# A forward scan moved ahead of the key product in a blocked linear attention, and weight splits and a sort moved ahead of the second expand group

## The chip, the cores and the metric

The kernel runs on one core of one Trainium2 chip. The metric is the device time of one execution in microseconds (us). A core has five engines with their own instruction streams: TensorE (PE, matrix products; PEld are its weight loads), VectorE (DVE), ScalarE (ACT), GpSimd (POOL) and SyncE (SP, which issues DMAs here). They wait for each other by semaphores.

## The reference, cut to what matters

Two stages in sequence. The first is a linear attention with a decaying state, for 4 batches, 8 heads, 768 steps and a head size of 48; the second a mixture of 8 experts in which each of the 3072 tokens goes to one.

```python
state = 0
for t in range(768):
    cur = einsum('bhd,bhe->bhde', u * k[t], v[t])
    y[t] = einsum('bhd,bhde->bhe', r[t], state + cur)
    state = w[t][..., None] * state + einsum('bhd,bhe->bhde', k[t], v[t])
x = y as [3072 tokens, 384]
logits = x @ w_gate
e = argmax(logits); g = softmax(logits)[e]
out = g * (relu(x @ w1[e]) @ w2[e])      # w1 384x1024, w2 1024x384
```

## The kernel before, in words

**Stage one, 24 blocks.** Time is cut into 12 chunks of 64 steps, and each chunk into two blocks (two batches each). A block holds 8 segments of 64 steps, so its tiles are 112 partitions by 512 columns. For block n VectorE makes two running products of the decay: a forward scan `pre` (`dve_pre`, L346, the scan at L351), whose segment ends are inverted by a small reciprocal (L354), and a backward scan `suf` (`dve_suf`, L356, the scan at L360), which reads those ends. Then `kh` = k times `suf` (`dve_kh`, L364, product at L368, VectorE) and `rh` = r times `pre` (`pool_rh`, L389, product at L393, GpSimd) feed TensorE: `pe_a` (L457) multiplies kh and rh into `ap`, and VectorE copies the part below the diagonal into `at` under a mask (`dve_at`, L370, L373). `at` times v is added to rh times the carried state (`pe_inter`, `pe_av`), and the state takes kh transposed times v (`pe_kt`, `act_kt`, `pe_dp`). GpSimd also makes `rk` = r times k (L387) and, from ScalarE's column `ct`, half of the diagonal of `at` (`pool_diag`, L421; ScalarE makes the other half, L430).

**The order.** The order of each engine is written out by hand: `iteration(n)` (L707) emits block n's products and the parts of blocks n+1 and n+2 that are made ahead, and each engine runs what it is given in that order. For VectorE one iteration is: `suf` of n+1; in every fourth iteration the gate or the place of a group of four blocks; `at` of n; `kh` of n+1; `pre` and its reciprocal for n+2. For GpSimd: `rh` of n+1, `rk` of n+2, from iteration 6 on the scatter of 128 finished tokens by an indirect DMA (L603), the diagonal of n+1, and once in four the copy of token numbers (L598). In iteration 3 GpSimd also builds a list of small constants (`late_constants`, L192).

**Routing.** As groups of four blocks are done, the gate's logits are taken (`logit_mm`, `logit_tr`, `gate`), each token's row among its expert's is counted on TensorE (`rank`, L568, its running base copied by ScalarE at L580) and turned into a row number (`place`, L582, VectorE), and the token is scattered to that row of `xs` in HBM. The expert with the most tokens is chosen early (`choose`) and is computed first; its first 256 rows (`ua`) come from groups that were counted by then, the other 208 (`ub_`) are loaded later. The order of the rest follows from a sort of the counts (`sort_experts`, L630: five small VectorE operations), and SP reads the second expert's number from its result (`expert_of`, L691) before it issues that expert's loads.

**The tail of stage one.** After the loop (from L854) the last block's products, the row transposes of `ua`, the last ranks and scatters and the first expert's expand groups are interleaved by hand. An expand group `mm1(ua, f)` (`expand`, L304) is nine products into one bank, a ScalarE relu `hh` (L313) and a VectorE residual `hl` (L314). Weights are split into a high and a low part before use: `side(0)` (L806) takes the next piece in a list and calls `split_part` (L230), a ScalarE copy (L237) and a VectorE subtraction (L239) on 128 x 512. For one expert the list has six pieces of w1, of which the first three serve f = 0 to 3 and the other three f = 4 to 7, then six of w2. When all pieces of a load are split, `feed` (L790) issues the next load. Then `contract` (L317) multiplies the eight `hh`, `hl` pairs with w2, 24 products to an output slice, and VectorE scales the slice (L330). After that comes the second part of the first expert, and then seven experts in the same way.

Of the kernel before, what the change touches and what calls it, by code (L numbers as in the profile page):

```python
# [22 lines left out]
NB = NS * 2  # L23
# [32 lines left out]
def rwkv_moe_kernel(ctx, tc, rkw, vv, ub, wg, wr, w1, w2, out):  # L56
# [18 lines left out]
    def work(shape, dtype, tag, name=None):  # L75
        return wk.tile(shape, dtype, name=name or tag, tag=tag, bufs=WKB[tag])
# [14 lines left out]
    def misc(name):  # L91
        return psM.tile([P, BANK], F32, name=name, tag="m")
# [241 lines left out]
    def prefill(e):  # L334
        nc.sync.dma_start(xs[e, LEAST:CMAX, :].rearrange("(p j) c -> p (j c)", j=ZJ), zrow[:(CMAX - LEAST) // ZJ])
# [4 lines left out]
    def real(n):  # L340
        return 0 <= n < NB
# [1 line left out]
    def part(j):  # L343
        return slice(64 * j, 64 * j + (64 if j == 0 else D))

    def dve_pre(n):  # L346
        if real(n):
            d = blk[n]
            d["pt"] = pre_[n % 2]
            d["pre"] = d["pt"][:, 0, 0:NW].rearrange("p (m c) -> p m c", c=SEG)  # L350
            nc.vector.tensor_tensor_scan(out=d["pt"][:, 0, 0:NW], data0=d["w"], data1=cell[:RP, 0:1].broadcast_to([RP, NW]),  # L351
                                         initial=1.0, op0=ALU.mult, op1=ALU.min)
            src = d["pt"][:, :, C + 1:C + 1 + NW].rearrange("p o (m c) -> p o m c", c=SEG)[:, :, :, 0]
            nc.vector.reciprocal(d["ends"], src.rearrange("p o m -> p m o"))  # L354

# [8 lines left out]
    def dve_kh(n):  # L364
        if real(n):
            d = blk[n]
            d["kh"] = work([RP, NSEG, C], F32, "kh")
            nc.vector.tensor_tensor(out=d["kh"], in0=d["k"], in1=d["suf"][:, :, 3:SEG], op=ALU.mult)  # L368
# [34 lines left out]
    def act_g(n):  # L403
        if real(n) and n >= 2:
            p = n % 2
            nc.scalar.activation(gst[p], U[:RP, p, 0:NSEG * D], AF.Copy)
# [115 lines left out]
    def pe_xT(n, t):  # L522
        if real(n):
            G, i = divmod(n, GRP)
            blk[n]["xp"] = xp = t[:, 0:DM]
            for j in range(3):
                nc.tensor.transpose(xp[:, j * P:(j + 1) * P], ch["xr", G][:, i, j * P:(j + 1) * P], ident)  # L527
# [12 lines left out]
    def logit_tr(k):  # L540
        lt = misc("lt")[:, 0:32 * k[2]]
        nc.tensor.transpose(lt, ch["ls"], ident[0:32 * k[2], 0:32 * k[2]])
        ch["lp", k] = lt.rearrange("p (b e) -> p b e", e=32)[:, :, 0:E]
# [24 lines left out]
    def rank(k):  # L568
        G, i, m = k
        oh = ch["r", k][0]  # L570
        t = misc("rank")
        rk = t[:, 0:(m + 1) * E].rearrange("p (b e) -> p b e", e=E)
        ch["rank", k] = rk
        nc.tensor.matmul(rk, one32, ch["base"].unsqueeze(1).broadcast_to([1, m + 1, E]), start=True, stop=False, skip_group_check=True)
        nc.tensor.matmul(rk[:, 0:m], tri, oh, start=False, stop=False, skip_group_check=True)
        for b in range(m):
            nc.tensor.matmul(rk[:, b + 1:], ones, oh[:, b:b + 1, :].broadcast_to([P, m - b, E]),
                             start=False, stop=(b == m - 1), skip_group_check=True)
        ch["base"] = nb = sm.tile([1, E], F32, name="base", tag="base", bufs=3)
        nc.scalar.activation(nb, rk[0:1, m, :], AF.Copy)  # L580
# [126 lines left out]
    def iteration(n):  # L707
        G, i = divmod(n, GRP)
        g = G - 1 if n >= 0 else -1
        whole = (g, 0, GRP)  # L710
        if 0 <= n < E // 2:
            prefill(2 * n)
            prefill(2 * n + 1)
        if n >= 0:
            load(n + 6)
        full = 0 <= g < NG - 1
        if real(n):
            blk[n]["ap"] = psA.tile([P, 4, 256], F32, name="ap", tag="ap")
            pe_xT(n - 1, blk[n]["ap"][:, 1:3, :].rearrange("p a c -> p (a c)"))
            pe_inter(n)  # L720
            if full and i == 1:
                logit_tr(whole)
            pe_a(n)
            if n == 0:
                zeros(blk[n]["yp"][:, 1, NQ * D:], 3)
        dve_scale(n + 1)
        act_pend(n + 1)
        act_g(n + 1)
        pool_rh(n + 1)
        dve_suf(n + 1)  # L730
        if full and i == 1:
            gate(whole)
        if full and i == 2:
            place(whole)
        if n == -2:
            pool_rk(0)
        pe_kt(n)
        act_pad(n + 2)
        if n == NB - 2:
            dve_kh(n + 1)  # L740
            dve_at(n)
            side()
        else:
            dve_at(n)
            dve_kh(n + 1)
        act_kt(n)
        act_ct(n + 1)
        if n > -2:
            pool_rk(n + 2)
        pe_av(n)  # L750
        if full and i == 0:
            act_xT(n - 1)
            logit_mm(whole)
        if n < 2:
            act_diag(n + 1, range(0, H if n < 0 else NQ))
        if n == NB - 2:
            dve_diag(n + 1)
            act_xT(n - 1)
            act_xr(n)
        else:  # L760
            act_xr(n)
            if not (full and i == 0):
                act_xT(n - 1)
        if 2 <= n < NB - 2:
            act_diag(n + 1, range(0, NQ))
        if moved(n) and n < NB - 2:
            scatter(*moved(n), ch["lp"] if full and i == 0 else ch["av"])
        if n >= 0:
            pool_diag(n + 1)
        dve_pre(n + 2)  # L770
        pe_dp(n)
        if n >= 0:
            load_v(n + LV)
        if n == FIRST * GRP + 6:
            choose()
            eid[0] = expert_of(first[0:1, 0:1])
            feed()
        if full and i == 1:
            weigh(whole)
            pool_ids(g)  # L780
            rank(whole)
        if n == 3:
            late_constants()
# [22 lines left out]
    def side(limit=E):  # L806
        if sides and sides[0][1] <= limit:
            kind, e, i, t, p, done = sides.pop(0)
            if kind == "split":
                split_part(wts[e % 2], t, i, p)  # L810
            else:
                check_w(e - 1, t, p)
            if done:
                out_.remove((e, i))
                feed()
# [33 lines left out]
    with tc.manual_schedule(engines={ET.PE, ET.DVE, ET.Activation, ET.Pool}):  # L849
# [6 lines left out]
        ua, z = ch["ua"], NB - 1  # L856
# [27 lines left out]
        def mm1(u, f):  # L884
            expand(wts[u["e"] % 2], f, u["x"], u["n"], u["hs"])
# [7 lines left out]
        penalty()  # L893
        scatter(last, (0, 1, 2))
        mm1(ua, 0)
        rank(kb)
        weigh(kb)
        place(kb)
        scatter(last, (3,))
        side(0)  # L900
        mm1(ua, 1)
        side(0)
        mm1(ua, 2)
        side(0)
        sort_experts()
        eid[1] = expert_of(order[0:1, 0:1])
        ub_ = rows_of(HB, HA, 0)
        feed()
        for f in range(3, 8):
            mm1(ua, f)  # L910
            side(0)
            if f == 5:
                check_counts()
        actx.close()
# [299 lines left out]
```

## Time and profile before

| | |
|---|---|
| median of 3 runs | 391.16 us (390.44 to 392.19) |
| the profiled execution's own time | 389.0 us |
| span of the profiled execution, first to last instruction | 387.3 us |
| mean granted TensorE clock | 0.974 |
| busy: PE / PEld / DVE / ACT / POOL | 360.6 / 326.1 / 261.6 / 196.0 / 143.8 us |
| chain that ended last, share by engine | PE 80%, DVE 7%, ACT 4%, issue 3%, POOL 2% |
| DMA | 67.63 MB, mean 175 GB/s |

The profile shows one execution. The chain is followed back from the last instruction: at each step to what released it, or to the instruction before it on its engine. A row of the timeline gives start (us from the span's start), duration (us), engine, line, operation, output<-inputs, form, count, and in brackets the engine's idle time before it with what ended it. A row of windows gives the busy time of each engine in a stretch, and the granted clock (PEclk; 1.00 is 2.4 GHz, 0.50 is 1.2 GHz). A row by line gives the count, total busy time, mean ns of one, idle time before them and what ended it. Matmul ends are modelled, so a busy TensorE is not TensorE at its peak.

### The profile page before, as it was taken

The numbers are of one execution on the slowest core, as the hardware profiler recorded it, in microseconds if no ns is written. First come the engines' busy times: TensorE is split into PE (matmuls) and PEld (weight loads), VectorE is DVE, ScalarE is ACT, GpSimd is POOL, SyncE is SP. The second block draws the span as 40 slices with busy tenths as digits, with TensorE's granted clock in tenths as the row PEclk, the third lists the DMA queues.
The fourth block names the chain that finished last, engine by engine and source line by source line (L and its number), as shares of the span: only waits on it lengthen the run. The fifth ranks groups of instructions, "written<-read, shape, count | busy, mean of one in ns | idle before, by whom it ended". The sixth has DMA issues, their size and how long they took to land.

```text
span 387.3 us, 11609 instructions
## 1 busy us (share of the span) xinstructions
PE 360.6 (93%) x4644; PEld 326.1 (84%) x4645; DVE 261.6 (68%) x451; ACT 196.0 (51%) x516; POOL 143.8 (37%) x195
## 2 busy tenths in 40 slices
PE   7988999999998896999999999999999999999991
PEld 5666777777776675998998999999999999999990
DVE  8789999989998436595665376476476585782410
ACT  3665666566666234374454355465565563751200
POOL 5577688788887171111000130130130262124021
PEclk9999999999999696999999999999999999999996
DMA  7997777677768125977444554754764665811001
GB/s 205 261 276 215 225 209 225 202 218 220 221 179 278 50 111 146 284 244 239 117 164 162 151 155 149 224 161 154 226 172 146 208 164 187 248 70 40 20 19 41
DMA packets 38021, 67.63 MB, mean 175 GB/s; under 512 B 8141, under 2 KB 19714, under 8 KB 37962
## 3 DMA queue, kind: packets, MB, share of 16 engines
q1 hardware_dynamic: 31658, 57.33, 50.2%
q0 software_dynamic: 6304, 9.50, 7.7%
q8 instruction: 38, 0.62, 0.7%
q14 instruction: 21, 0.17, 0.1%
HBM read 55.34 MB, written 11.64 MB: 173 GB/s over the span
## 4 chain that ended last, share of the span: by engine, by line
PE 80%; DVE 7%; ACT 4%; issue 3%; POOL 2%; another core or an unknown queue 1%; DMA 1%; POOLq 0%; DVEq 0%; ACTq 0%
PE N L311 15%; PE N L325 14%; PE cell L311 7%; PE mM L311 6%; PE N L994 6%; PE cell L994 4%; PE mM L994 3%; PE yp L489 3%; PE yp L479 3%; PE ap L464 2%; DVE kh L368 2%; PE U L499 2%; PE N L300 2%; PE ap L527 2%; PE wrm L142 2%
## 5 line engine op out<-in xcount | busy, mean ns | idle before, releaser
L275 POOL DMA_INDIRECT out_dram<-ot,gi x16 | 22.2, 1391 | 104.0 <-issue 71.7
L275 POOL DMA_INDIRECT out_dram<-ort,gi x13 | 15.5, 1195 | 76.9 <-issue 19.3
L325 PE MATMUL N<-w2h,hh 128*128 128x384 f32 (+4 forms) x104 | 35.9, 345 | 0.0
L314 DVE SCALAR_TENSOR_TENSOR hl<-N,hh 128x256 fp32r<-128x256 f32 (+8 forms) x38 | 19.8, 522 | 23.7 <-ACT hh L313 21.9
L325 PE MATMUL N<-w2l,hh 128*128 128x384 f32 (+4 forms) x104 | 35.0, 337 | 0.0
L325 PE MATMUL N<-w2h,hl 128*128 128x384 f32 (+4 forms) x104 | 35.0, 337 | 0.0
L239 DVE TENSOR_TENSOR w2l<-wst,w2h 128x512 fp32r<-128x512 f32 x48 | 32.1, 687 | 4.1 <-ACT w2h L237 3.6
L239 DVE TENSOR_TENSOR w1l<-wst,w1h 128x512 fp32r<-128x512 f32 x48 | 33.1, 690 | 1.4 <-ACT w1h L237 1.0
L387 POOL TENSOR_TENSOR rk<-rkwt 112x512 f32<-112x512 f32 x24 | 30.6, 1275 | 7.8 <-DMA rkwt<-in_rkw_dram 7.8
L603 POOL DMA_INDIRECT xs<-xr,pi x24 | 24.7, 1028 | 23.8 <-issue 7.3
L313 ACT ACTIVATE hh<-N 128x256 fp32r<-128x256 f32 (+8 forms) x38 | 17.6, 464 | 27.0 <-PE N L311 22.4
L360 DVE TENSOR_TENSOR_SCAN suf<-rkwt,cell 112x536 f32<-112x536 f32 x24 | 30.4, 1267 | 0.5
L237 ACT ACTIVATE w2h<-wst 128x512 fp32r<-128x512 f32 x48 | 28.5, 625 | 3.5 <-DMA wst<-in_w_dram 3.5
L351 DVE TENSOR_TENSOR_SCAN pre<-rkwt,cell 112x536 f32<-112x536 f32 x24 | 30.2, 1259 | 0.2 <-DMA rkwt<-in_rkw_dram 0.2
L237 ACT ACTIVATE w1h<-wst 128x512 fp32r<-128x512 f32 x48 | 29.8, 623 | 0.2 <-ACT x L301 0.2
L393 POOL TENSOR_TENSOR rh<-rkwt,pre 112x512 f32<-112x512 f32 x24 | 28.9, 1203 | 2.3 <-DVE pre L351 2.0
L311 PE MATMUL N<-xh,w1h 128*128 128x440 f32 (+6 forms) x84 | 28.8, 343 | 0.0
L311 PE MATMUL N<-xh,w1l 128*128 128x440 f32 (+6 forms) x84 | 28.6, 341 | 0.0
L311 PE MATMUL N<-xl,w1h 128*128 128x440 f32 (+6 forms) x84 | 28.6, 340 | 0.0
L368 DVE TENSOR_TENSOR kh<-rkwt,suf 112x512 f32<-112x512 f32 x24 | 28.4, 1181 | 0.0
L430 ACT ACTIVATE at<-id,ct 128x64 f32<-128x64 f32 x96 | 25.3, 343 | 0.1
L373 DVE COPY_PREDICATED at<-cmask,ap 128x512 f32<-128x512 int32 x24 | 17.6, 735 | 10.2 <-PE ap L464 7.6
(200 smaller groups left out, 967.5 us busy)
## 6 DMA issues: line engine op xcount, KB each, us to landing
wst<-in_w_dram SPq DMA_DIRECT2D x48, 256.0 KB
wst<-in_w_dram SPq DMA_DIRECT2D x16, 768.0 KB
rkwt<-in_rkw_dram SPq DMA_DIRECT2D x72, 96.0 KB
rkwt<-in_rkw_dram SPq DMA_DIRECT2D x24, 238.0 KB
vt<-in_vv_dram SPq DMA_DIRECT2D x48, 96.0 KB
wck_t<-in_wr_dram SPq DMA_DIRECT2D x6, 768.0 KB
rkwt<-in_rkw_dram SPq DMA_DIRECT2D x12, 224.0 KB
xg<-xs SPq DMA_DIRECT2D x4, 579.0 KB
```

Source lines behind the costliest of these rows:

```text
L237: nc.scalar.activation(hi, st[:, cs], AF.Copy)
L239: nc.vector.tensor_tensor(out=lo, in0=st[:, cs], in1=hi.bitcast(F32), op=ALU.subtract)
L275: i = nc.gpsimd.indirect_dma_start(out=out[:, :], out_offset=bass.IndirectOffsetOnAxis(ap=t.bitcast(I32)[0:rows.shape[0], q, 1:2], axis=0) ...
L311: nc.tensor.matmul(hp, a, x[p][:, j, :], start=(i == 0), stop=(i == 8))
L325: nc.tensor.matmul(op, a[:, cs], w2v(wt, w, f), start=(i == 0), stop=(i == 23))
L351: nc.vector.tensor_tensor_scan(out=d["pt"][:, 0, 0:NW], data0=d["w"], data1=cell[:RP, 0:1].broadcast_to([RP, NW]), initial=1.0, op0=ALU.mu ...
L360: nc.vector.tensor_tensor_scan(out=suf[:, ::-1], data0=d["w"][:, ::-1], data1=cell[:RP, 0:1].broadcast_to([RP, NW]), initial=1.0, op0=ALU. ...
L368: nc.vector.tensor_tensor(out=d["kh"], in0=d["k"], in1=d["suf"][:, :, 3:SEG], op=ALU.mult)
L387: nc.gpsimd.tensor_tensor(out=d["rk"], in0=d["r"], in1=d["k"], op=ALU.mult)
L393: nc.gpsimd.tensor_tensor(out=d["rh"], in0=d["r"], in1=d["pre"][:, :, 1:C + 1], op=ALU.mult)
L430: nc.scalar.activation(d["at"][:, h // NQ, h % NQ, :], id2, AF.Copy, scale=d["ct"][:, h:h + 1])
L994: nc.tensor.matmul(pp, w, a, start=(i == 0), stop=(i == 23))
```

## The change

In `iteration`, for n from 2 to 21, VectorE's `kh` of block n+1 moves behind the forward scan of block n+2: `at`, scan, `kh`, reciprocal instead of `at`, `kh`, scan, reciprocal. The other engines' orders in the loop stay as they are. In the tail, three calls of `side(0)` (the three pieces of w1 that serve f = 4 to 7) move from between the expand groups 1 to 3 to behind `mm1(ua, 0)`, ahead of the last rank; and the sort, the reading of the second expert's number, the load of `ub_` and the `feed` move ahead of expand group 1. Nothing is computed otherwise than before.

```diff
--- before.py
+++ after.py
@@ -343,13 +343,16 @@
     def part(j):
         return slice(64 * j, 64 * j + (64 if j == 0 else D))
 
-    def dve_pre(n):
+    def dve_pre(n, m):
         if real(n):
             d = blk[n]
             d["pt"] = pre_[n % 2]
             d["pre"] = d["pt"][:, 0, 0:NW].rearrange("p (m c) -> p m c", c=SEG)
             nc.vector.tensor_tensor_scan(out=d["pt"][:, 0, 0:NW], data0=d["w"], data1=cell[:RP, 0:1].broadcast_to([RP, NW]),
                                          initial=1.0, op0=ALU.mult, op1=ALU.min)
+        if 2 <= m < NB - 2:
+            dve_kh(m + 1)
+        if real(n):
             src = d["pt"][:, :, C + 1:C + 1 + NW].rearrange("p o (m c) -> p o m c", c=SEG)[:, :, :, 0]
             nc.vector.reciprocal(d["ends"], src.rearrange("p o m -> p m o"))
 
@@ -742,7 +745,8 @@
             side()
         else:
             dve_at(n)
-            dve_kh(n + 1)
+            if n < 2:
+                dve_kh(n + 1)
         act_kt(n)
         act_ct(n + 1)
         if n > -2:
@@ -767,7 +771,7 @@
             scatter(*moved(n), ch["lp"] if full and i == 0 else ch["av"])
         if n >= 0:
             pool_diag(n + 1)
-        dve_pre(n + 2)
+        dve_pre(n + 2, n)
         pe_dp(n)
         if n >= 0:
             load_v(n + LV)
@@ -893,22 +897,20 @@
         penalty()
         scatter(last, (0, 1, 2))
         mm1(ua, 0)
+        for _ in range(3):
+            side(0)
         rank(kb)
         weigh(kb)
         place(kb)
         scatter(last, (3,))
-        side(0)
-        mm1(ua, 1)
-        side(0)
-        mm1(ua, 2)
-        side(0)
         sort_experts()
         eid[1] = expert_of(order[0:1, 0:1])
         ub_ = rows_of(HB, HA, 0)
         feed()
-        for f in range(3, 8):
+        for f in range(1, 8):
             mm1(ua, f)
-            side(0)
+            if f > 2:
+                side(0)
             if f == 5:
                 check_counts()
         actx.close()
```

## Rows read from the trace of the kernel before

**Rows 1.** Windows: busy us of each engine in three stretches, granted clock, DMA
```profile
core 0: us, PE busy (x) PEld busy (x) DVE busy (x) ACT busy (x) POOL busy (x), PEclk, DMA share, GB/s
47.90:120.20 72.30, 68.57 (x1935) 54.46 (x1927) 68.08 (x98) 47.01 (x165) 58.41 (x74) 1.00 0.73 212
...
149.05:155.88 6.83, 6.18 (x26) 5.74 (x27) 5.95 (x19) 4.09 (x11) 0.00 (x0) 0.50 0.54 181
156.80:182.00 25.20, 25.20 (x175) 24.74 (x174) 17.51 (x34) 13.63 (x30) 3.38 (x4) 1.00 0.84 261
```

**Rows 2.** Windows, line L368 (kh) alone: busy us and count on DVE
```profile
47.90:120.20 72.30, 17.67 (x14) 1.00 0.73 212
```

**Rows 3.** Groups by line, VectorE: forward scan and masked copy
```profile
L351 DVE TENSOR_TENSOR_SCAN pre<-rkwt,cell 112x536 f32<-112x536 f32 x24 | 30.2, 1259 | 0.2 <-DMA rkwt<-in_rkw_dram 0.2
...
L373 DVE COPY_PREDICATED at<-cmask,ap 128x512 f32<-128x512 int32 x24 | 17.6, 735 | 10.2 <-PE ap L464 7.6 <-ACT at L430 1.5 <-ACT ex L565 1.0
```

**Rows 4.** Timeline of a steady block (n = 11), VectorE and GpSimd
```profile
68.67 0.74 DVE L373 COPY_PREDICATED at<-cmask,ap 128x512 f32<-128x512 int32 x1 [0.24 <-PE ap L464]
...
69.03 1.27 POOL L387 TENSOR_TENSOR rk<-rkwt 112x512 f32<-112x512 f32 x1
...
69.31 1.54 DVE L368 TENSOR_TENSOR kh<-rkwt,suf 112x512 f32<-112x512 f32 x1
...
70.58 1.17 POOL L603 DMA_INDIRECT xs<-xr,pi  x1 [0.28 <-PE yp L489]
```

**Rows 5.** Timeline of iterations 3 and 4, VectorE and GpSimd
```profile
28.44 1.26 DVE L351 TENSOR_TENSOR_SCAN pre<-rkwt,cell 112x536 f32<-112x536 f32 x1
...
29.83 0.29 POOL L194 TENSOR_SCALAR_AFFINE_SELECT tri<-tri 128x128 bf16<-128x128 bf16 x1
...
31.99 1.17 POOL L393 TENSOR_TENSOR rh<-rkwt,pre 112x512 f32<-112x512 f32 x1
...
32.30 3.20 DVE L368 TENSOR_TENSOR kh<-rkwt,suf 112x512 f32<-112x512 f32 x1
...
33.13 1.26 POOL L387 TENSOR_TENSOR rk<-rkwt 112x512 f32<-112x512 f32 x1
...
34.35 0.60 POOL L421 TENSOR_TENSOR at<-id,ct 128x256 f32<-128x256 f32 x1
...
35.43 1.25 DVE L351 TENSOR_TENSOR_SCAN pre<-rkwt,cell 112x536 f32<-112x536 f32 x1
...
36.77 1.19 POOL L393 TENSOR_TENSOR rh<-rkwt,pre 112x512 f32<-112x512 f32 x1 [1.81 <-DVE pre L351]
```

**Rows 6.** Timeline of iteration 5, VectorE and GpSimd
```profile
38.60 0.74 DVE L373 COPY_PREDICATED at<-cmask,ap 128x512 f32<-128x512 int32 x1
...
39.23 0.69 DVE L368 TENSOR_TENSOR kh<-rkwt,suf 112x512 f32<-112x512 f32 x1
...
40.27 0.61 POOL L421 TENSOR_TENSOR at<-id,ct 128x256 f32<-128x256 f32 x1 [1.09 <-ACT ct L411]
...
40.83 0.19 POOL L598 COPY xr<-tokid 128x4 int32<-128x4 int32 x1
```

**Rows 7.** Timeline of the tail, from the last rank's base to the first scaled slice
```profile
145.05 0.17 ACT L580 ACTIVATE base<-rank 1x8 f32<-1x8 f32 x1 [3.22 <-PE N L311]
...
148.74 0.38 ACT L313 ACTIVATE hh<-N 128x256 fp32r<-128x256 f32 x1 [3.01 <-remote]
...
149.16 0.42 DVE L314 SCALAR_TENSOR_TENSOR hl<-N,hh 128x256 fp32r<-128x256 f32 x1 [2.70 <-ACT hh L313]
...
149.70 0.80 PE L311 MATMUL N<-x,w1h 128*128 128x256 f32 x2 [2.80 <-ACT w1h L237]
...
156.78 0.34 PE L325 MATMUL N<-w2h,hh 128*128 128x384 f32 x1
...
157.97 1.29 DVE L239 TENSOR_TENSOR w2l<-wst,w2h 128x512 fp32r<-128x512 f32 x2
...
161.15 0.62 DVE L330 TENSOR_SCALAR ort<-N,gi 128x384 f32<-128x384 f32 x1 [1.88 <-PE N L325]
```

**Rows 8.** Waits of SP's queue, 110 to 160 us: total, times, longest
```profile
SPq L692 <- DVE order L637: 5.3, 1, 5.3
```

## The prediction

> **What bounds the kernel now.** The chain that ended last lies mostly on TensorE, and next on VectorE (the table ahead has the shares), so time is won only where TensorE waits, or where VectorE hands it work late. Next I read busy time by stretch [rows 1]. Through blocks 8 to 21 of the loop (47.9 to 120.2 us) VectorE is busy 68.08 and TensorE 68.57 of 72.30 us: two engines in step, neither with much to give. At 149.05 to 155.88 the granted clock is 0.50, so TensorE runs at 1.2 GHz instead of 2.4. From 156.8 to 182 TensorE is busy the whole 25.20 us, so what starts that stretch earlier moves the end by as much. In the same blocks fourteen products that make the keys (kh) take 17.67 us [rows 2], 1.26 each, while a single one takes 0.69 [rows 6]; the forward scan takes 1259 ns on average [rows 3].
>
> The timeline of a steady block tells why [rows 4]. GpSimd's product rk runs 69.03 to 70.30; VectorE's kh starts at 69.31 and ends at 70.85, 0.55 after rk. kh stands still while GpSimd multiplies; scans keep their length. Where GpSimd issues products back to back, kh waits for all of them [rows 5]: started at 32.30 it sat through rh, rk and the diagonal and ended at 35.50, again 0.55 after the last (34.95).
>
> **The change, part by part.** The sum is made against the profiled execution, 389.0 us (span 387.3); the median of the runs is 391.16, so I add 2.16 at the end.
>
> Part one, steady blocks. No instruction is added or removed; kh swaps places with a scan of 1.26 us. kh would be asked for some 1.9 us after the start of the masked copy (at) instead of 0.64: in [rows 4] at 70.57, when rk is done and GpSimd is at its scatter, so it takes about 0.69 there. Over the fourteen the excess is 17.67 - 14 x 0.69 = 8.0 us [rows 2]. That is the upper end, as if VectorE alone set the pace. It does not: at already waits for the attention products in 7.6 of its 10.2 idle us [rows 3], and TensorE is idle only 72.30 - 68.57 = 3.7 us [rows 1]. The lower end is 0: TensorE keeps its pace. I take 3.0, near TensorE's idle time, because TensorE is late next. What waits behind the later kh: the reciprocal, then the backward scan, on VectorE; the attention products of the next block on TensorE, two us later in [rows 4] than kh's end, so covered. The scan asks earlier for a column that ScalarE pads; a tenth of a us a block at most, as an estimate, inside this range.
>
> Part one, first blocks. The first scatter comes in iteration 6; before it GpSimd has nothing between a diagonal and the next rh but a wait for the scan: rh at 36.77 waited 1.81 us for the scan of 35.43 [rows 5]. Moving that scan forward removes the wait, so GpSimd runs on without a gap, and kh, now behind the scan, meets the whole run. Iteration 4: the scan runs 32.30 to 33.56; kh asks while rk is running (33.13 to 34.39); the diagonal follows to 34.95, then rh (1.19) to 36.1 and the next rk (1.26) to 37.4; kh ends at 37.9. Before, kh and scan were both done at 36.68: 1.2 us lost. Iteration 5 [rows 6]: the diagonal starts 1.67 after at (38.60), held by ScalarE's ct, not by VectorE. The new kh asks 0.63 + 1.25 = 1.88 after at, 0.2 too late to be first. Diagonal, token copy, rh and rk last 0.61 + 0.19 + 1.19 + 1.26 = 3.25; kh ends 1.67 + 3.25 + 0.55 = 5.5 after at, where kh and scan now end 1.32 + 1.25 = 2.5 after it: 3.0 lost, and the next at waits for it through kh, backward scan and place. Sum: 4.2 lost. In iterations 2 and 3 I count 0: small operations there should let kh in. Bounds: a gain of 1.4 (case a) to a loss of 9.4 (case c).
>
> Here a rule weighs against the row. The Trainium skill, page "SBUF — State Buffer", section "Who interferes with whom", says a VectorE instruction with two SBUF inputs contends with a GpSimd instruction that reads SBUF, and that whoever issues first keeps the pair for the whole instruction. By it kh would lose to one instruction only; the row of 32.30 shows three, and I go by the row.
>
> Part two, the tail. Three splits (each a ScalarE copy and a VectorE subtraction, some 0.65 apiece) and the sort (small VectorE operations) move ahead of the second expand group. Now ScalarE idles 3.22 us until 145.05 and 3.01 until 148.74, the first behind TensorE; VectorE gets its next residual at 149.16, and TensorE waits 2.80 for a split of w1 until 149.70, then runs at half clock [rows 7, 1]. After: the splits lie in ScalarE's and VectorE's first idle time (142 to 145), so groups four and five follow at once and no split of w1 stands between the residuals. If the two late results stay late, VectorE has from 149.16 seven residuals (0.42) and six splits of w2 (0.645, from the pair of 1.29): 6.8 us, to 156.0. The last six of the 24 products of the first output slice come after that. A product takes (161.15 - 156.78) / 24 = 0.18, so the slice is scaled at 157.1 instead of 161.15 [rows 7]. Gain 4.0. If the late results come in time too, VectorE starts some 3 us sooner: gain up to 7. Lower end 0: the waits come back at group six, which needs a bank that the residual of group one frees. I take 4.0, nearest to the rows as they stand.
>
> Moved queues: SP waits 5.3 us for the sort's order [rows 8]; behind it stand the second row load, then the second expert's weights. They go out some 4 us earlier, which I cost at nothing, as TensorE is never short of data from 156.8 on [rows 1]. GpSimd's last scatter waits for a place that now stands behind three splits; with that result seen at 145.05 anyway it costs 0; if not, 2 us under the contraction's cover.
>
> **Sum:** -3.0 + 4.2 - 4.0 = -2.8. 389.0 - 2.8 = 386.2 profiled, 388.3 as the median.
>
> **The rivals.** (a) GpSimd's products let kh in between them: iteration 4 ends at 34.39 + 0.55 = 34.95 instead of 36.68 (1.7 gained), iteration 5 loses 0.3; the first blocks gain 1.4 instead of losing 4.2: 382.7. Against it: kh behind three [rows 5]. For it: that run was a backlog after a list of small constants. Chance 0.17. The page's rule above would give this.
>
> (b) The tail gives nothing, since the two late results only move to the next instruction that needs them: -3.0 + 4.2 = +1.2, 392.3. For it: ScalarE's 3.01 us has no releaser that the profile names [rows 7]. Against it: the splits need no result of TensorE. Chance 0.2.
>
> (c) Slower: the same blocking in iteration 3. There small constants (one of 0.29 at 29.83 that reads SBUF) follow the diagonal, then rh at 31.99 and rk to 34.39 [rows 5]. If these hold kh off as well, it ends at 34.95, where kh and scan now end at 29.70: 5.2 more, 393.5. It decides if kh, asking at about 29.2, finds no gap up to 31.99. Against it: the constants are short. Chance 0.13.
>
> (d) The swap does nothing in steady blocks because TensorE keeps its pace: 388.3 + 3.0 = 391.3. Chance 0.08.
>
> **How the numbers follow.** The forecast has 0.42. 0.5%, about what a measurement of this kernel tells from no change, is 2.0 us: faster is below 389.2, slower above 393.1. Faster: 0.36 of the forecast's 0.42 (its bounds spread it by 2 us either way), all 0.17 of (a), 0.03 of (b) and (d): 0.56. Slower: half of (c), a third of (b), 0.02 of the rest: 0.15. Same: 0.29. The range goes from (a) to just short of (c): 382.7 to 393.0.
>
> **What would show it.** Right: kh near 0.7 from iteration 7 on, beside scatters; kh of over 3 us in iterations 4 and 5; at waiting for attention products in most steady blocks; no wait of 2.80 us at the fourth group; the first output slice scaled about 4 us earlier against the end of the loop. Wrong: kh short everywhere (a), one of some 5 us in iteration 3 (c), TensorE still idle before the contraction (b).

## The result, and the profile after

The changed kernel takes 390.56 us (median of 21 runs, 383.31 to 396.55), the kernel before 391.16 in its three first runs and 391.2 over the 21 taken beside it. The ratio is 0.9896, with a 95% interval of 0.9861 to 0.9932: about 4 us faster by that ratio. The ratios here count only the runs within 1.5% of the fastest of their own kernel, here 9 of 21 after and 16 of 21 before, and so lean on how fast that fastest one happened to be: over all 21 runs the medians differ by 0.6 us only, the means by 2.0. The profiled execution went from 389.0 to 386.4 us, its span from 387.3 to 384.7.

Cut into stages, the 2.6 us of the two spans are a sum of large terms with opposite signs. "at(n)" is the start of VectorE's masked copy of block n; every boundary is read from a timeline.

| stage | before | after | difference |
|---|---|---|---|
| start to at(0) | 12.6 | 13.1 | +0.5 |
| at(0) to at(8), first blocks | 41.0 | 44.1 | +3.1 |
| at(8) to at(20), steady blocks | 61.0 | 61.6 | +0.6 |
| at(20) to at(23), end of the loop | 18.4 | 16.3 | -2.1 |
| at(23) to the first scaled output slice, tail | 28.1 | 21.6 | -6.5 |
| from there to the end | 226.2 | 228.0 | +1.8 |

The page of the changed kernel: busy time by engine, and the granted clock in 40 slices.

```profile
PE 360.2 (94%) x4645; PEld 325.4 (85%) x4645; DVE 252.7 (66%) x451; ACT 195.1 (51%) x516; POOL 149.5 (39%) x195
...
PEclk9995999999999999999999999999999999999996
```

VectorE lost 8.9 us of busy time (261.6 before), TensorE none. The 5 in the fourth slice is a half-clock stretch that the kernel before did not have at that place; its own stretches lay near the end of the loop (125 to 129 and 132 to 135 us, which goes with the 2.1 us of the fourth stage) and in the tail [rows 1].

**Steady blocks.** Windows of the changed kernel, in the columns of [rows 1]: at(7) to at(21), its counterpart, and the half-clock stretch.

```profile
52.70:125.70 73.00, 68.95 (x1935) 54.28 (x1927) 60.30 (x98) 46.84 (x165) 61.90 (x75) 1.00 0.74 219
27.14:37.38 10.24, 10.12 (x206) 8.23 (x204) 4.50 (x6) 4.82 (x17) 5.42 (x24) 0.50 0.79 224
```

VectorE has 7.8 us less to do in the same fourteen blocks (68.08 to 60.30), yet they take 73.0 us instead of 72.3. TensorE's busy time has hardly moved (68.57 to 68.95). The groups of VectorE in this stretch show where the 7.8 us went.

```profile
L376 DVE COPY_PREDICATED at<-cmask,ap 128x512 f32<-128x512 int32 x14 | 10.5, 748 | 5.9 <-PE ap L467 4.2 <-PE yp L513 1.0 <-ACT ex L568 0.7
L371 DVE TENSOR_TENSOR kh<-rkwt,suf 112x512 f32<-112x512 f32 x14 | 9.8, 698 | 0.0
...
L562 DVE TENSOR_REDUCE mx<-lt 128x4 f32<-128x32 f32 x4 | 0.8, 192 | 5.4 <-PE lt L545 5.4
```

The keys (kh) cost 0.70 each instead of 1.26 [rows 2], as foreseen. But the time went into waits for TensorE: 5.9 us ahead of the masked copy (5.2 of them TensorE's) and 5.4 ahead of the gate's maximum. Before, in the same fourteen blocks, it was 1.4 and 1.8; the first of the two:

```profile
L373 DVE COPY_PREDICATED at<-cmask,ap 128x512 f32<-128x512 int32 x14 | 10.2, 732 | 1.4 <-ACT ex L565 0.7 <-PE ap L464 0.6
```

One steady block, in the place of [rows 4]:

```profile
73.51 1.27 POOL L390 TENSOR_TENSOR rk<-rkwt 112x512 f32<-112x512 f32 x1
73.59 1.27 DVE L351 TENSOR_TENSOR_SCAN pre<-rkwt,cell 112x536 f32<-112x536 f32 x1
74.77 0.67 DVE L371 TENSOR_TENSOR kh<-rkwt,suf 112x512 f32<-112x512 f32 x1
74.94 1.38 POOL L606 DMA_INDIRECT xs<-xr,pi  x1 [0.17 <-issue]
```

The scan runs beside rk and keeps its length; kh comes when rk is over and runs 0.67 beside the scatter.

**First blocks.** Timeline of iterations 2 to 4, in the place of [rows 5].

```profile
25.73 0.80 PE L492 MATMUL yp<-vt,at 64*64 64x48 f32 x32 [1.47 <-DMA rkwt<-in_rkw_dram]
...
30.48 0.73 DVE L376 COPY_PREDICATED at<-cmask,ap 128x512 f32<-128x512 int32 x1 [2.87 <-PE ap L467]
...
37.49 0.76 DVE L376 COPY_PREDICATED at<-cmask,ap 128x512 f32<-128x512 int32 x1 [2.79 <-PE ap L467]
...
39.39 1.00 DVE L371 TENSOR_TENSOR kh<-rkwt,suf 112x512 f32<-112x512 f32 x1
...
39.81 1.64 POOL L396 TENSOR_TENSOR rh<-rkwt,pre 112x512 f32<-112x512 f32 x1
```

Here kh is not starved: it takes 1.00 and GpSimd's rh is the one held up (1.64 instead of 1.18). TensorE waited 1.47 us at 25.73, ran at half clock from 27.14 to 37.38, and the masked copy waited 2.87 and 2.79 us for it. So this profile loses in the first blocks, but not by the predicted mechanism.

**Tail.** Timeline from the splits of w1 to the first scaled slice, in the place of [rows 7].

```profile
143.86 1.67 ACT L237 ACTIVATE w1h<-wst 128x512 fp32r<-128x512 f32 x3
...
144.51 1.90 DVE L239 TENSOR_TENSOR w1l<-wst,w1h 128x512 fp32r<-128x512 f32 x3
...
147.85 0.17 ACT L583 ACTIVATE base<-rank 1x8 f32<-1x8 f32 x1 [2.33 <-PE N L311]
148.72 0.94 ACT L313 ACTIVATE hh<-N 128x256 fp32r<-128x256 f32 x3 [0.71 <-remote]
...
149.16 1.07 DVE L314 SCALAR_TENSOR_TENSOR hl<-N,hh 128x256 fp32r<-128x256 f32 x3
...
156.71 0.62 DVE L330 TENSOR_SCALAR ort<-N,gi 128x384 f32<-128x384 f32 x1 [1.09 <-PE N L325]
```

The late results of TensorE (ScalarE and VectorE get what a product made only some us after TensorE has issued it and gone on) are still there (base at 147.85, hh of the second group at 148.72), but the splits are done before them, and three hh and three hl follow without a gap. TensorE no longer waits 2.80 us for a split, and the half-clock stretch of the tail [rows 1] is gone.

**After the tail.** One group of ScalarE's waits from 157 to 176 us, and TensorE's wait behind it.

```profile
ACT w2h L237 <- DMA wst<-in_w_dram: 4.2, 2, 2.4
```
```profile
174.21 0.42 PE L325 MATMUL N<-w2h,hh 128*104 128x384 f32 x1 [0.97 <-ACT hh L313]
174.99 0.43 PE L325 MATMUL N<-w2h,hl 128*104 128x384 f32 x1 [0.36 <-DVE hl L314]
```

The contraction now runs into the next limit: the second expert's weights have not landed when ScalarE wants to split them, and 1.3 us of the gain go back at 174.21. The kernel before had no such wait. SyncE issued these weights at 154.29, and before the change at 154.37, while the slice comes 4.4 us sooner. The second row load and those weights stand behind GpSimd's last scatter, which started at 149.19 instead of 146.39. The scatter, and SyncE's issue after and before:

```profile
149.19 0.97 POOL L606 DMA_INDIRECT xs<-xr,pi  x1 [1.78 <-ACT hh L313]
...
154.29 3.08 SPq L224 DMA_DIRECT2D wst<-in_w_dram  x6
```
```profile
154.37 3.10 SPq L224 DMA_DIRECT2D wst<-in_w_dram  x6
```

### The profile page after: what moved, and what is told of

It is laid out like the page before. It is cut to its first block, busy times and chain, and to the rows that moved or that the text cites. A ratio compares the mean times of both kernels' runs of the same rounds, so it can differ in the third digit from the quotient of the medians.

```text
span 384.7 us, 11608 instructions
## 1 busy us (share of the span) xinstructions
PE 360.2 (94%) x4645; PEld 325.4 (85%) x4645; DVE 252.7 (66%) x451; ACT 195.1 (51%) x516; POOL 149.5 (39%) x195
## 4 chain that ended last, share of the span: by engine, by line
PE 79%; DMA 6%; DVE 5%; ACT 4%; issue 2%; SPq 1%; POOL 0%; POOLq 0%; ACTq 0%; DVEq 0%
PE N L311 13%; PE N L325 11%; PE N L996 6%; PE cell L311 6%; PE mM L311 6%; DMA wst<-in_w_dram 4%; PE yp L482 4%; PE U L502 4%; PE cell L996 4%; PE mM L996 3%; PE ap L467 3%; PE yp L492 3%; PE ap L530 3%; PE kp L519 3%; DMA rkwt<-in_rkw_dram 3%
## 5 line engine op out<-in xcount | busy, mean ns | idle before, releaser
L606 POOL DMA_INDIRECT xs<-xr,pi x24 | 27.8, 1158 | 20.8 <-PE lp L537 4.1
L396 POOL TENSOR_TENSOR rh<-rkwt,pre 112x512 f32<-112x512 f32 x24 | 29.8, 1241 | 1.6 <-DVE pre L351 1.6
L302 DVE TENSOR_TENSOR xl<-N,xh 128x440 fp32r<-128x440 f32 (+6 forms) x21 | 11.8, 566 | 16.4 <-ACT xh L301 16.3
```

Source lines behind the costliest of these rows:

```text
L396: nc.gpsimd.tensor_tensor(out=d["rh"], in0=d["r"], in1=d["pre"][:, :, 1:C + 1], op=ALU.mult)
L606: i = nc.gpsimd.indirect_dma_start(out=xsf, out_offset=bass.IndirectOffsetOnAxis(ap=ch["pi", G, b], axis=0), in_=xr[:, b, :], in_offset=No ...
```

## The experiments

Twelve kernels in three groups; the kernels of a group shared one chip and their runs of the kernel before. The second and third group ran on the same chip, the first on another. My theory at the start: the gain lies in the tail, the steady blocks give nothing since TensorE sets their pace, and the first blocks lose. The rivals: the early loss is only a chance half-clock stretch, or the tail is worth little.

### First group: one part at a time

**Part one alone** (as in the change; the tail as before):

```diff
-            dve_kh(n + 1)
+            if n < 2:
+                dve_kh(n + 1)
...
+        if 2 <= m < NB - 2:
+            dve_kh(m + 1)
```

> Part one alone (the forward scan ahead of the keys from block 2 on; the tail as it was before). Theory: kh takes 0.67 in the steady blocks instead of 1.26, but the masked copy then waits for the attention products, so at(8) to at(21) stays within 1.5 us of the 66.6 of before; the first blocks lose 1 to 4 us; time 391 to 395 us, a ratio of 1.000 to 1.010. Rival: the loss of the first blocks in the changed kernel's profile (at(8) at 57.2 instead of 53.6) belongs to its half-clock stretch and not to the new order, and the shorter keys are worth something: 387 to 390 us, a ratio of 0.990 to 0.997.

Measured: 387.85 us (before: 386.0), ratio 0.9916, interval 0.9864 to 0.9968. The ratio goes with the rival and the medians with the theory, so for the time this run settles nothing: by the medians of all runs it is 1.9 us slower, by the ratio 0.8% faster. at(8) to at(21) took 70.5 us, outside the theory's band around the first chip's 66.6; but the kernel before takes 70.3 there too on another chip (the kernel before again, below). The profile holds the starved kh that I had predicted for iteration 4. Its timeline:

```profile
33.48 1.26 POOL L390 TENSOR_TENSOR rk<-rkwt 112x512 f32<-112x512 f32 x1
33.69 4.54 DVE L371 TENSOR_TENSOR kh<-rkwt,suf 112x512 f32<-112x512 f32 x1
34.70 0.60 POOL L424 TENSOR_TENSOR at<-id,ct 128x256 f32<-128x256 f32 x1
35.28 1.18 POOL L396 TENSOR_TENSOR rh<-rkwt,pre 112x512 f32<-112x512 f32 x1
36.42 1.26 POOL L390 TENSOR_TENSOR rk<-rkwt 112x512 f32<-112x512 f32 x1
```

kh asked while rk ran, sat through the diagonal, rh and the next rk (to 37.68), and ended 0.55 after that, at 38.23.

**Part two alone** (blocks as before; the diff of the tail as in the change):

```diff
         mm1(ua, 0)
+        for _ in range(3):
+            side(0)
         rank(kb)
...
-        for f in range(3, 8):
+        for f in range(1, 8):
```

> Part two alone (splits, sort and second expert's number ahead of the second expand group; every block as it was before). Theory: the whole gain of the change lies here; from at(23) to the first scaled output slice 21 to 23 us instead of 28.1; time 384.5 to 387.5 us, a ratio of 0.983 to 0.991, not slower than the whole change. Rival: the tail is worth some 2 us only, since the interval of 28.1 in the kernel before was long for a half-clock stretch of that one execution; ratio 0.993 to 0.997.

Measured: 386.0 us (386.0), ratio 0.9981, interval 0.9936 to 1.0026. The ratio misses theory and rival, though its interval reaches into the rival's band: on this chip no gain of the tail shows. From at(23) to the first slice this kernel takes 21.0 us, as the theory says, but the old tail of part one alone takes 19.9 (138.61 to 158.51) here, and not 28.1. The rows of that old tail show why.

```profile
146.77 0.17 ACT L583 ACTIVATE base<-rank 1x8 f32<-1x8 f32 x1 [0.31 <-PE rank L580]
...
148.00 0.38 ACT L313 ACTIVATE hh<-N 128x256 fp32r<-128x256 f32 x1 [0.54 <-PE N L311]
...
158.51 0.62 DVE L330 TENSOR_SCALAR ort<-N,gi 128x384 f32<-128x384 f32 x1 [1.40 <-PE N L325]
```

ScalarE waits 0.31 and 0.54 us where it waited 3.22 and 3.01 before [rows 7]. The late results are missing in all four profiles of this chip.

**New order from block 7 on only, with the new tail:**

```diff
-        if 2 <= m < NB - 2:
+        if 7 <= m < NB - 2:
...
-            if n < 2:
+            if n < 7:
```

> The whole change, but with the new order of VectorE only from block 7 on, where every block has a scatter; blocks 2 to 6 keep the old order. Theory (the new order costs 1 to 4 us in the first blocks and nothing later): at(7) to within 1 us of the 47.95 of before, time 383 to 386 us, a ratio of 0.980 to 0.988, faster than the whole change (0.990). Rival (the first blocks lose to TensorE's half clock, whatever the order): the same as the whole change within 1 us, 0.987 to 0.992.

Measured: 384.9 us (386.0), ratio 1.0027, interval 0.9989 to 1.0065; the tail takes 20.0. Not the theory's 0.980 to 0.988, which counted on a gain of the tail that this chip does not have, nor the rival's 0.987 to 0.992. at(7) came at 51.8, and not within 1 us of 47.95, behind a half-clock stretch from 26 to 30.

**The three splits alone, sort left in its place:**

```diff
         mm1(ua, 0)
+        for _ in range(3):
+            side(0)
         rank(kb)
...
-        side(0)
         mm1(ua, 1)
-        side(0)
         mm1(ua, 2)
-        side(0)
         sort_experts()
```

> Of part two only the three splits move ahead of the rank of the last tokens; sort and second expert's number stay behind the third expand group, and the blocks are as before. Theory: the gain of the tail comes from the splits, as TensorE then has no wait for w1 at the fourth group: within 1 us of part two alone. Rival: the sort, left between the residuals of the first groups and behind the late results of TensorE, costs 1.5 to 3 us more than part two alone, because VectorE and the transfers that wait for the second expert's number start later.

Measured: 387.46 us (386.0), ratio 0.9993, interval 0.994 to 1.0046; the tail takes 20.0. That is 1.1 us less than part two alone and even with the kernel above, so the sort's place costs nothing here, but where nothing is late this can't tell what matters.

### Second group: is it the late results?

**The whole change again,** unaltered.

> The whole change, unaltered, beside the kernel before, on the chip that this group of runs gets. Theory: the gain of the first measurement hangs on the late results of TensorE in the tail (the kernel before and the whole change both show them there; the four one-part kernels don't); where they are absent the interval from at(23) to the first scaled slice is about 20 us in either kernel, the first blocks lose some 3 us and the steady blocks give nothing, so the ratio is 1.000 to 1.010; where they are present, 0.985 to 0.993. Rival: the change gains its 1 percent on any chip, and the one-part kernels are only within their own scatter: 0.986 to 0.993 with an interval of 20 us as well.

Measured: 390.75 us (391.59), ratio 0.9934, interval 0.9883 to 0.9985. Late results are present: ScalarE waits 2.87 us for the second group's, and the tail takes 25.1, not the rival's 20. The ratio lies a hair above both bands.

**The kernel before again,** unaltered.

> The kernel before, unaltered, for its profile on this chip and as a measure of the scatter: a ratio of 0.995 to 1.005. Theory: no late results in the tail here, so from at(23) to the first scaled slice 19 to 21 us (28.1 in the first profile) and no wait of ScalarE above 2.5 us in it behind TensorE's expand groups. Rival: the late results belong to the old tail, and show here as well: 25 us or more.

Measured: 390.36 us (391.59), ratio 0.9975, interval 0.9927 to 1.0023. On this chip the late results are there in the old tail as well, as the rival said. The timeline, in the place of [rows 7]:

```profile
145.35 0.17 PE L577 MATMUL rank<-oh,ones 128*128 128x8 bf16 x1
...
149.45 0.17 ACT L580 ACTIVATE base<-rank 1x8 f32<-1x8 f32 x1 [2.46 <-PE N L311]
...
152.44 0.38 ACT L313 ACTIVATE hh<-N 128x256 fp32r<-128x256 f32 x1 [2.31 <-remote]
...
153.40 0.50 PE L311 MATMUL N<-x,w1h 128*128 128x256 f32 x2 [2.10 <-ACT w1h L237]
...
164.09 0.62 DVE L330 TENSOR_SCALAR ort<-N,gi 128x384 f32<-128x384 f32 x1 [1.91 <-PE N L325]
```

The rank's last product starts at 145.35, ScalarE takes its result 4.1 us later; TensorE, which has gone on, then stands 2.10 us for a split that queues behind the late hh. From at(23) at 137.37 to the slice: 26.7 us. So it is not the order of the tail alone that decides, but whether results come late.

**TensorE itself late, old tail:**

```diff
+        zeros(N[1], 24)
         rank(kb)
         weigh(kb)
```

> The kernel before, with 24 products of zeros (128x512, about 0.21 us each, 5.1 in all) on TensorE between the first expand group and the rank of the last tokens, so that rank and second group come 5 us late for every engine. Theory: the old tail has nothing else ready for VectorE and ScalarE at that place, so the whole 5 us show: from at(23) to the first scaled slice 24 to 26 us. Rival: the contraction has that much slack, and it stays under 22.

**TensorE itself late, new tail** (the same line, in part two alone):

```diff
+        zeros(N[1], 24)
         rank(kb)
```

> The same 24 products of zeros at the same place, in part two alone (the new tail). Theory: the three splits of w1 (about 2 us of VectorE) run while rank and second group are late, so the interval from at(23) to the first scaled slice is 1.5 to 2.5 us shorter than with the old tail and the same zeros: 22 to 24 us. Rival 1: all of the lateness is hidden, under 21. Rival 2: none of it, within 0.7 us of the old tail.

Measured, in one execution each, by a row of the products of zeros, the slice, and in the first also the rank and its base; at(23) is at 134.19 and 131.67.

```profile
141.69 5.13 PE L142 MATMUL N<-wz,ones 128*128 128x512 bf16 x23
...
147.11 0.17 PE L577 MATMUL rank<-oh,ones 128*128 128x8 bf16 x1
...
147.93 0.17 ACT L580 ACTIVATE base<-rank 1x8 f32<-1x8 f32 x1 [4.09 <-PE rank L577]
...
159.11 0.62 DVE L330 TENSOR_SCALAR ort<-N,gi 128x384 f32<-128x384 f32 x1 [1.41 <-PE N L325]
```
```profile
139.18 5.13 PE L142 MATMUL N<-wz,ones 128*128 128x512 bf16 x23
...
156.60 0.62 DVE L330 TENSOR_SCALAR ort<-N,gi 128x384 f32<-128x384 f32 x1 [1.78 <-PE N L325]
```

24.92 and 24.93 us: the old tail lies in its theory's band, and the new one hides nothing, against my theory and for rival 2. Where TensorE itself is late, it is the bound behind the lateness, seven groups and a contraction without a gap, and the splits are never what it waits for. What the new order helps against is something else: TensorE has gone on, and the engines that feed it see its results late.

These two runs show one thing more. Behind the zeros no result is late, on the chip where the unaltered tails have them: the rank's last product starts at 147.11 and ScalarE takes it 0.8 us later, not 4.1 (0.8 in the new tail too, 144.60 to 145.39). Ahead of the zeros the first of the two still had a late result: hh of its first group waited 1.75 us. So 5.1 us of useless products left the old tail 1.8 us shorter than the unaltered one of the kernel before again (24.92 against 26.72). The lateness goes with what TensorE does ahead of it, or with the moment, and not with the chip alone; one execution each doesn't tell which.

### Third group: late takers, and the two halves of part one

**ScalarE busy, old tail:**

```diff
+        for _ in range(9):
+            nc.scalar.activation(dly, wz, AF.Copy)
         rank(kb)
```

> The kernel before, with nine copies (128x512, about 0.55 us each, 5.0 in all) that nobody reads on ScalarE between hh of the first expand group and the copy of base: TensorE goes on by itself, but its results are taken some 5 us late, as in the first profile. Theory: in the old tail the splits of w1 queue behind that, TensorE finishes groups two to four's first three and then waits some 3 to 5 us for a split of w1, and the interval from at(23) to the first scaled slice goes from 20 to 24.5 to 26 us. Rival: the interval stays under 22.5, since ScalarE and VectorE catch up.

**ScalarE busy, new tail** (six copies, as the splits ahead of them fill the rest):

```diff
+        for _ in range(6):
+            nc.scalar.activation(dly, wz, AF.Copy)
         rank(kb)
```

> Part two alone, with six such copies (3.3 us) at the same place, which the three splits now precede, so that the results are again taken some 5 us late. Theory: TensorE has its splits of w1 and runs groups two to six without a wait of over 1 us; VectorE's seven residuals and six splits of w2 then set the end: 21 to 22.5 us, 2.5 to 4 less than the old tail with its copies. Rival: the lateness costs the new tail as much as the old one, a difference under 1 us.

Measured, one execution each, old tail (at(23) at 139.80) and then new tail (at(23) at 134.62):

```profile
147.81 5.92 ACT L898 ACTIVATE dly<-wz 128x512 bf16<-128x512 bf16 x9
...
154.36 0.80 PE L312 MATMUL N<-x,w1h 128*128 128x256 f32 x2 [3.12 <-ACT w1h L238]
...
166.18 0.62 DVE L331 TENSOR_SCALAR ort<-N,gi 128x384 f32<-128x384 f32 x1 [1.93 <-PE N L326]
```
```profile
145.24 3.93 ACT L900 ACTIVATE dly<-wz 128x512 bf16<-128x512 bf16 x6
...
150.84 0.50 PE L312 MATMUL N<-x,w1h 128*128 128x256 f32 x2 [0.70 <-DVE order L638]
...
157.85 0.62 DVE L331 TENSOR_SCALAR ort<-N,gi 128x384 f32<-128x384 f32 x1 [1.06 <-PE N L326]
```

26.4 and 23.2 us, 0.4 and 0.7 above their bands, where a copy took 0.66 and not 0.55. The difference is 3.1, inside the theory's 2.5 to 4 and against the rival, but not all of it is the wait: TensorE ran at half clock from 153.3 to 160.1 in the old tail and not behind 138 in the new one. Its last three groups took 4.4 us there (27 products, 157.33 to 161.76), and would take 3.2 at the pace of the first run with zeros (63 products in 7.55 us), so some 1.2 us, as an estimate, are clock; the 1.9 left lie between rival and theory. The wait for w1 at the fourth group comes back in the old tail (3.12 us) and is not there in the new one, whose longest wait is 0.70. That is the mechanism of the tail, made by hand: not late results as such, but splits that queue behind the late takers while TensorE stands.

The clock follows the same line. In all four old tails with late results or late takers the wait for w1 (2.80, 2.10, 3.12, and 3.46 in the early-only kernel below) has a half-clock stretch of 3.4 to 6.8 us that begins within about 1 us of its end; of the four new ones two have a stretch behind the rank, of 3.4 us; of the six tails without lateness none has. Whether the wait brings the stretch is not shown.

**The new order in iterations 2 to 6 only,** old tail:

```diff
-        if 2 <= m < NB - 2:
+        if 2 <= m < 7:
...
-            if n < 2:
+            if n < 2 or n >= 7:
```

> The forward scan ahead of the keys in the iterations 2 to 6 only; all later blocks and the tail as before. Theory: the loss of part one lies here: from at(0) to at(8) 44 to 47 us (41 to 44.5 in the kernels with the old order), kh(5) of over 4 us where it meets a run of GpSimd's products; time 0.5 to 3 us above the kernel before, a ratio of 1.001 to 1.008. Rival: no difference in the first blocks that exceeds the scatter, at(0) to at(8) under 43.5, a ratio within 0.997 to 1.003.

Measured: 394.64 us (392.35), ratio 1.0129, interval 1.0034 to 1.0224, from six runs. By the ratio it is slower by more than the theory says; the medians over all runs lie 0.6% apart, inside the theory's band. at(0) to at(8) is 43.2 us, under the theory's band and under the rival's bound as well, so the stage as a whole doesn't separate them. Single blocks do. VectorE's timeline, with one row of GpSimd's:

```profile
32.81 0.74 DVE L376 COPY_PREDICATED at<-cmask,ap 128x512 f32<-128x512 int32 x1 [1.03 <-PE ap L467]
...
34.68 4.39 DVE L371 TENSOR_TENSOR kh<-rkwt,suf 112x512 f32<-112x512 f32 x1
...
40.86 0.73 DVE L376 COPY_PREDICATED at<-cmask,ap 128x512 f32<-128x512 int32 x1
...
42.53 0.61 POOL L424 TENSOR_TENSOR at<-id,ct 128x256 f32<-128x256 f32 x1 [4.01 <-ACT ct L414]
...
42.66 1.03 DVE L371 TENSOR_TENSOR kh<-rkwt,suf 112x512 f32<-112x512 f32 x1
...
45.47 0.75 DVE L376 COPY_PREDICATED at<-cmask,ap 128x512 f32<-128x512 int32 x1
```

kh(5) is starved for 4.39 us and the block from at(4) to at(5) takes 8.05. In the ten kernels with the old order in these blocks it takes 6.9 to 7.1 in nine (kh(5) 2.65 to 3.21; the tenth was at half clock just before). The next one, at(5) to at(6), takes 4.61 as in the kernel before (4.62).

**New order from block 7 on only, with the new tail,** again (the edit of the first group's third kernel):

> Again the whole change with the new order of VectorE from block 7 on only, on the chip of this group. Theory: as the whole change without its loss in the first blocks: where the results of TensorE come late in the tail, a ratio of 0.980 to 0.990; where they don't, 0.994 to 1.001. Rival: not better than the whole change was: 0.990 to 1.003 on any chip.

Measured: 388.13 us (392.35), ratio 0.9869, interval 0.9809 to 0.9929; with late results, a tail of 24.1 us, and so within the theory's band for that case. It is the best version found. On the chip without late results it was even with the kernel before (1.0027). That it beats the whole change is likely but not shown: they were never timed in one group, and the intervals overlap.

## Why the prediction was right, and where its steps were not

The forecast was 2.9 us faster (388.3 against 391.16); measured are about 4 us by the ratio of 0.9896 and 0.6 by the medians, both within the range. The total was right; of its three terms one was wrong and two were right in part, and that their errors cancel is luck: about 2 us too much gain in the steady blocks against about 3 us too much loss in the first ones.

**Steady blocks, predicted -3.0: about -1.** The step that failed is "I take 3.0, near TensorE's idle time". That VectorE's excess disappears was right (1.26 to 0.70 per kh), and so was what is late next. The 7.6 of 10.2 us that it cites [rows 3] are of all 24 blocks; in the fourteen, at waited 1.4 us only, so there VectorE nearly set the pace, and behind it TensorE was next at no distance. TensorE's idle time did not shrink when VectorE handed over sooner: 3.7 us before [rows 1], 73.0 - 68.95 = 4.05 after. At full clock, at(8) to at(20) took 61.0 to 63.1 us in six kernels with the old order there and 61.6 to 63.4 in four with the new. Rival (d), which had a chance of 0.08, holds in these blocks. One block does gain: from at(7) to at(8), 5.7 to 5.9 in eight of nine kernels with the old order (5.1 in the kernel before again, just out of a half-clock stretch), 4.4 to 4.7 in the new, as the kh of that block, held 2.0 to 2.3 us in the eight, comes down to 0.7 to 1.1.

**First blocks, predicted +4.2: +1.2 at full clock.** Of the two steps, iteration 4 was right to the tenth: predicted 1.2 lost with a kh that ends 0.55 behind the second rk; shown in three of the four kernels with the new order here (4.54, 4.54 and 4.39 us; at(4) to at(5) 8.05 to 8.19 against 6.92). Iteration 5 failed: "0.2 too late to be first" was right (kh came 0.13 behind the diagonal's start, 42.66 against 42.53), but kh did not then wait for the whole run. It ended 0.55 after the diagonal alone, and GpSimd's next instruction waited for it; in part one alone and the whole change again that kh took 0.67 and met nothing. The changed kernel's profile shows the same at 39.39, and its 3.1 us were lost where TensorE ran at half clock: at(2) to at(4) took 14.2 us instead of 8.9. Half clock also came right behind the starved kh in two of its three profiles (at 40.2 and 43.5 us), so the price of iteration 4 may be above 1.2; that is not shown.

So neither the row of [rows 5] nor the rule I weighed against it holds throughout. The Trainium skill, page "SBUF — State Buffer", section "Who interferes with whom", says that whoever issues first keeps the pair for that whole instruction. The kh of 39.39, 45.25 and 42.66 fit that; the kh of 33.69 lost to three more products in a row and does not. In these profiles kh went next wherever it came up during the diagonal. Where it came up during rk it sometimes waited out the run, and sometimes went next as well: at 18.80 in the changed kernel it ended 0.55 after rk, and the diagonal behind was held (1.06 instead of 0.60). What decides is open.

**Tail, predicted -4.0: -6.5 in the two first profiles, 0 on the chip of the first group, -2.8 on that of the later ones.** The mechanism held: splits in the idle time ahead of late results, no wait of TensorE at the fourth group. What the prediction did not know is that the lateness is no property of the kernel. Without it old and new tail take 19.9 and 20.0 us; with it 26.7 and 28.1 against 25.1 and 24.1 on the chip of the later groups (means of 27.4 and 24.6), and 28.1 against 21.6 in the first pair. Rival (b), the tail gives nothing, is true where nothing is late. From the second group's residual to the slice, the stretch that the prediction priced at 4.0, the old tails with late results took 12.0, 11.2 and 12.1 us and the new ones 7.6, 8.6 and 8.7; the old ones hold 6.8, 3.4 and 6.8 us of half clock, the new ones 0, 3.4 and 3.4, so a part of this gain is clock. The first pair came near the bound of -7 because that residual also came 2.1 us sooner after at(23) in its new tail (14.1 instead of 16.1).

**Moved queues, predicted 0: +1.3 of the 1.8 us lost after the tail.** The failed step is "TensorE is never short of data from 156.8 on". That was so in the kernel before because its tail was slow. "They go out some 4 us earlier" failed with it: they went out at the same time (154.29 and 154.37), behind a scatter that started 2.8 us later. So they had 2.4 us up to the first slice instead of 6.8, and were late. It is no fixed cost: TensorE waits 0.4 to 1.0 us in the same place in the kernels of the first group, with the old tail too, and not at all in the whole change again.

**The sum.** With +1.2 for iteration 4, -1.2 for the block at(7) to at(8), 0 for the rest and -2.8 for the tail, the chip of the second group should show -2.8 us, a ratio of 0.993; it showed 0.9934. For the first measurement, -6.5 and +1.8 in place of -2.8 give -4.7, a ratio of 0.988, against 0.9896. The first group's chip should then show part two at 1.000 (0.9981) and part one at 1.000, where 0.9916 was measured; and the new order in the early blocks alone should lose 1.2 us, where 1.0129 is 5. Neither ratio is borne out by all runs of its kernel. As an estimate at equal clock (a straight line through the times and mean granted clocks of all runs of a group, without two of 485 and 486 us; each 0.01 goes with some 3 us) part one alone differs from the kernel before by -0.5 us, part two alone by +0.2, the early blocks alone by +1.1, the whole change again by -1.7, and block 7 on with the new tail by -0.7 on the first chip and -2.8 on the second, each give or take 1.0 to 1.5 (the kernel before again, the same code, by +0.6). That fits the terms above within its scatter, with less for the tail, a part of whose gain is clock. For the first measurement this can't be done, since the clocks of the kernel before are not on record there.

## What to carry over

Where two engines run in step, the time that one of them gets back is worth only what the other is waiting for: VectorE's 7.8 us bought about 1. An independent piece of work belongs ahead of the wait that may be long, not behind it, since in the good case it cost the tail next to nothing here (20.0 to 21.0 us against 19.9) and in the bad case it fills the wait. And a wait read from one profile should be looked for in a second execution on another chip before it is priced: here a term as large as the whole forecast was there in some profiles only.

## What was not expected of the hardware

- **Results seen late.** In the tail ScalarE took a small product's result 2.6 to 4.8 us after TensorE had issued it, while TensorE went on with the next groups (145.35 and 149.45 in the kernel before, again). It shows in all six profiles of the old and the new tail in the first pair and on the chip of the later groups, and in none of four on the chip of the first group (ScalarE waits 0.31 and 0.54 us there); behind 5.1 us of zeros on TensorE it is absent on the later chip too (0.8 us). It is no wait for code: in the kernel before no instructions were loaded from 138 to 154 us. What holds the results back was not found.
- **Half clock by chance.** Executions of one kernel had their half-clock stretches at different places: the kernel before at 125 to 129, 132 to 135 and 149 to 156 us in one profile, at 45 to 52 and 154 to 158 in the other. In part one alone the stretch from 40.2 to 53.8 came right behind the starved kh, after which TensorE had waited, and in the whole change again one from 43.5 to 50.3; in the early-only kernel the same starvation was followed by none. So the wait alone doesn't decide it, and the scatter of single runs (379.6 to 392.6 us for part one alone) is several times the effect that was looked for.
